# Seven block products for the MLP's first matrix product, and its output sums kept in DRAM

## The chip, the cores and the metric

The kernel runs on one core of a Trainium2 chip. A core has five engines with an instruction queue each: TensorE (PE in the profile, with its weight loads shown as PEld), VectorE (DVE), ScalarE (ACT), GpSimd (POOL) and SyncE (SP), which issues the transfers. Each queue is worked off strictly in order. TensorE reads on-chip memory (SBUF) and adds its results up in PSUM, which has eight banks; VectorE and ScalarE empty these. Transfers between DRAM and SBUF run on 16 DMA engines. The metric is the time of one execution on the device, in microseconds (us).

## The reference

The input x is 2048 rows of 576 numbers. With xn the layer-normalised x, the output is

```
x + Cr @ (xn @ Dr^T) - Ci @ (xn @ Di^T) + relu(xn @ w1) @ w2
```

where Cr, Ci (2048 x 2048) and Dr, Di (576 x 576) are cosine and sine matrices that come as inputs, w1 is 576 x 4608 and w2 is 4608 x 576. All is in single precision. The last term is called the MLP here: `xn @ w1` its first products, `relu(...) @ w2` its second products.

## The kernel before

Single precision is made from half precision: each operand is split into a high and a low float16 part, and a product is three matmuls (high x high, high x low, low x high). `split` (L164) makes the two parts, the high one on ScalarE (L166), the low one on VectorE (L167), after a scaling by a power of two that is found from the largest magnitude (`magnitude`, L97; `power`, L101, which sends it through GpSimd's `partition_all_reduce`, L105).

The 2048 rows are four groups g of 512 (xT[g] holds the transposed, split xn of one group), the 4608 hidden columns are nine blocks b of 512. A step n is one pair (b, g), in the order of `steps` (L604): all four groups of block 0, then of block 1, and so on. In step n the kernel computes the first products of (b, g) and, woven between them, the second products of the step before.

- First products (L305, `mlp1_step`): four PSUM tiles of 128 hidden columns by 512 rows. Each takes 13 matmuls that stream 512 columns (L292), and four matmuls of 64 rows (L317) do the remainder of the depth 576 = 4 x 128 + 64. `mlp1_out` (L325) empties the tiles of two such products into h: the four blocks of 128 x 256 after relu, and four sums of them (S1 to S4), each as high and low part.
- Second products (L347, `mlp2`): the 2 x 2 blocks of each product are multiplied as seven block products instead of eight (Strassen's scheme in Winograd's form, the table `PRODUCTS`, L269). Each has 12 matmuls that stream 288 columns (L357), into two PSUM tiles of pool ps2. After each of the seven, VectorE adds the PSUM tile, scaled, to the sums in SBUF (L363, tiles acc, which began as x itself, so that the residual is in them). After block 8 the sums go to DRAM (tiles spill), and come back when the output is put together (L853).
- Preparation of the next block is a list of small pieces that `work` (L607) takes one by one between the products: loads of w1 and w2, magnitudes, splits, and the sums of w2's blocks (L440).
- `passes` (L676) take the largest magnitudes of the sequence matrices, one 512 KB load and one ScalarE pass (L672) at a time, in the MLP's steps.

In block 0 the groups are also normalised (`normalize`, L221), their low parts are taken on GpSimd (`remainder`, L229) and transposed on TensorE (`transposes`, L238). After the MLP follow the two DFT stages: `dft1` (L747) and the loop from L857, with seven block products too. They take some 440 us and are not touched, but for how the sums are loaded.

Instructions are written in program order; a scheduler orders each engine's queue and places the waits. `issue_after` pins an instruction behind another one of the same engine. Pools hand out buffers: a tile is written only when the one that had the buffer before has been read for the last time.

## Time and profile before

| | |
|---|---|
| median of 3 runs | 1283.71 us (1282.86 to 1283.82) |
| the profiled execution | 1283.83 us, of which the span of instructions is 1282.0 us |
| PE busy | 1264.8 us, 99% |
| DVE busy | 980.5 us, 76% |
| ACT busy | 539.0 us, 42% |
| POOL busy | 36.5 us, 3% |
| mean granted TensorE clock | 0.997 of full speed |

How to read the profile: a row of groups has the line, the engine and operation, output<-inputs, shapes and count, then busy time in us and the mean of one in ns, and behind the bar the idle time before them and who ended it. A row of a timeline has start, duration (both us), engine, line, operation and count, and in brackets the idle time before it with its releaser. Operations of one engine overlap, so what one costs in a queue is the distance from start to start, which is a little less than its duration. In rows of stretches the columns are the stretch, its length, the busy time (with the number of instructions) of PE, PEld, DVE, ACT and POOL, the granted clock, the DMA share and GB/s.

### The profile page before, as it was taken

How to read it: one execution, taken by the hardware profiler on the slowest of the kernel's cores; microseconds unless marked ns; L12 is line 12 of the kernel's file. 1: busy time of each engine (PE TensorE's matmuls, PEld its weight loads, DVE VectorE, ACT ScalarE, POOL GpSimd, SP SyncE). 2: the span in 40 equal slices, each digit the busy share in tenths (PEclk: the TensorE clock that was granted, in tenths of full speed). 3: DMA queues.
4: the chain of work that ended last, by engine and by line, in shares of the span. 5: the costliest groups of instructions: out<-in, count | busy, mean ns of one | idle time of the engine just before them, and what ended most of it. 6: DMA issues, size and time to landing. Idle time of an engine off the chain costs nothing.

```text
span 1282.0 us, 21851 instructions
## 1 busy us (share of the span) xinstructions
PE 1264.8 (99%) x9164; PEld 859.2 (67%) x9164; DVE 980.5 (76%) x1671; ACT 539.0 (42%) x794; POOL 36.5 (3%) x60
## 2 busy tenths in 40 slices
PE   8799999999999999999999999999999999999998
PEld 7565665666565665666565665677777777777777
DVE  8978877786686687777867868568678788888875
ACT  5834443343443443434434434244443333333332
POOL 2310000000000000000000000000000000000000
PEclk8999999999999999999999999999999999999999
DMA  6102112221221222122222213330033435334320
GB/s 243 43 1 68 56 59 91 86 77 65 87 91 68 64 79 68 69 91 87 69 73 86 97 57 110 112 132 17 1 114 124 155 101 167 121 125 133 130 85 19
DMA packets 38002, 112.75 MB, mean 88 GB/s; under 512 B 3984, under 2 KB 10640, under 8 KB 37904
## 3 DMA queue, kind: packets, MB, share of 16 engines
q1 hardware_dynamic: 37904, 111.36, 25.9%
q8 instruction: 71, 1.16, 0.4%
q14 instruction: 27, 0.22, 0.0%
HBM read 101.91 MB, written 9.44 MB: 87 GB/s over the span
## 4 chain that ended last, share of the span: by engine, by line
PE 91%; DVE 5%; ACT 1%; DMA 1%; issue 1%; SPq 0%; POOL 0%; POOLq 0%; ACTq 0%; DVEq 0%
PE p L292 29%; PE p L357 27%; PE p L872 26%; PE pd L760 7%; PE p L317 1%; DVE acc L363 1%; DVE w2s L167 1%; DVE xn L226 0%; DVE w1s L167 0%; DMA acc<-in_x_dram 0%; DVE st L184 0%; DMA c<-in_cre_dram 0%; DVE h L336 0%; PE pd L770 0%; ACT xn L227 0%
## 5 line engine op out<-in xcount | busy, mean ns | idle before, releaser
L292 PE MATMUL p<-xT,w1s 128*128 128x512 f16 (+1 forms) x2136 | 434.7, 355 | 1.3 <-ACT xT L249 1.1
L357 PE MATMUL p<-w2s,h 128*128 128x288 f16 x3024 | 394.6, 286 | 2.0 <-ACT xT L252 1.0
L357 PEld LDWEIGHTS <-h 128*128 128x128 f16 x3024 | 295.3, 98 | 103.0 <-issue 2.8
L872 PE MATMUL p<-R,cs 128*128 128x288 f16 x2688 | 329.4, 286 | 0.0
L292 PEld LDWEIGHTS <-w1s 128*128 128x128 f16 x2136 | 193.5, 98 | 201.9 <-issue 18.4
L872 PEld LDWEIGHTS <-cs 128*128 128x128 f16 x2688 | 263.0, 98 | 66.3
L363 DVE SCALAR_TENSOR_TENSOR acc<-p,c_ub,acc 128x576 f32<-128x576 f32 x252 | 204.8, 813 | 39.0 <-PE p L357 38.5
L166 ACT ACTIVATE cs<-c,sc_c 128x1024 f16<-128x1024 f32 x112 | 128.5, 1148 | 200.2 <-PE p L872 147.5
L167 DVE SCALAR_TENSOR_TENSOR cs<-c,sc_c,cs 128x1024 f16<-128x1024 f32 x112 | 143.7, 1283 | 50.3 <-ACT cs L166 50.1
L336 DVE SCALAR_TENSOR_TENSOR h<-p,h 128x256 f16<-128x256 f32 (+1 forms) x144 | 79.8, 555 | 94.8 <-ACT h L335 94.5
L342 ACT ACTIVATE h<-s 128x1024 f16<-128x1024 f32 x72 | 76.1, 1057 | 160.5 <-DVE s L340 160.4
L335 ACT ACTIVATE h<-p 128x256 f16<-128x256 f32 (+1 forms) x144 | 69.9, 486 | 147.2 <-PE p L292 141.4
L343 DVE TENSOR_TENSOR h<-s,h 128x1024 f16<-128x1024 f32 x72 | 88.1, 1224 | 31.2 <-ACT h L342 30.2
L760 PE MATMUL pd<-dsp,xT 128*128 128x288 f16 x832 | 104.0, 286 | 0.2
L760 PEld LDWEIGHTS <-xT 128*128 128x128 f16 x832 | 80.7, 98 | 22.6 <-issue 2.5
L878 DVE SCALAR_TENSOR_TENSOR o<-p,us_c,o 128x288 f32<-128x288 f32 x112 | 57.6, 514 | 20.3 <-PE p L872 20.3
L672 ACT ACTIVATE f<-f 128x1024 f32<-128x1024 f32 x64 | 66.6, 1041 | 3.7 <-DMA f<-in_cre_dram 3.7
L332 ACT ACTIVATE s<-p 128x256 f32<-128x256 f32 x72 | 27.4, 380 | 74.0 <-PE p L317 54.5
L166 ACT ACTIVATE w2s<-raw_w,c_sw 128x576 f16<-128x576 f32 (+1 forms) x54 | 44.2, 851 | 25.9 <-DVE raw_w L445 15.4
L167 DVE SCALAR_TENSOR_TENSOR w2s<-raw_w,c_sw,w2s 128x576 f16<-128x576 f32 (+1 forms) x54 | 48.5, 916 | 7.6 <-ACT w2s L166 7.6
L167 DVE SCALAR_TENSOR_TENSOR w1s<-raw_w,c_sw,w1s 128x640 f16<-128x640 f32 x36 | 30.8, 892 | 9.8 <-ACT w1s L166 9.8
L166 ACT ACTIVATE w1s<-raw_w,c_sw 128x640 f16<-128x640 f32 x36 | 27.9, 817 | 24.0 <-DVE c_sw L109 23.6
(106 smaller groups left out, 672.5 us busy)
## 6 DMA issues: line engine op xcount, KB each, us to landing
f<-in_cre_dram SPq DMA_DIRECT2D x32, 512.0 KB, 3.5
f<-in_cim_dram SPq DMA_DIRECT2D x32, 512.0 KB, 3.5
c<-in_cre_dram SPq DMA_DIRECT2D x32, 512.0 KB, 4.0
c<-in_cim_dram SPq DMA_DIRECT2D x32, 512.0 KB, 4.6
raw_w<-in_w_dram SPq DMA_DIRECT2D x17, 640.0 KB, 4.0
raw_w<-in_w_dram SPq DMA_DIRECT2D x18, 576.0 KB, 3.8
acc<-in_x_dram SPq DMA_DIRECT2D x16, 288.0 KB, 7.4
spill<-acc SPq DMA_DIRECT2D x16, 288.0 KB, 2.5
```

Source lines behind the costliest of these rows:

```text
L166: nc.scalar.activation(hi, src, AF.Copy, scale=s)
L167: nc.vector.scalar_tensor_tensor(lo, src, s, hi, ALU.mult, ALU.subtract)
L292: nc.tensor.matmul(ps[:, cols], w1s[b, i // 2][:, hl, i % 2 * KT + k], xT[g][:, kx, cols], start=(start and n == 0), stop=(stop and n == l ...
L335: nc.scalar.activation(hi, src, AF.Relu)
L336: stt(lo, src, 0.0, hi, ALU.max, ALU.subtract)
L342: order["s"] = nc.scalar.activation(hi, st[:, 1:], AF.Copy).ins
L343: order["lo"] = nc.vector.tensor_tensor(lo, st[:, 1:], hi, ALU.subtract).ins
L357: nc.tensor.matmul(ps[:, c], h[:, x, qa, c * P : (c + 1) * P], w[:, y, qb], start=first and i == 0 and j == 0, stop=i == NQ - 1 and j == 2 ...
L363: order["acc"] = nc.vector.scalar_tensor_tensor(o, ps, us[b], o, ALU.mult, ALU.add).ins
L672: nc.scalar.activation(f, f, AF.Abs, scale=2.0**-10, accum_out=sums_c[:, n, q : q + 1])
L760: nc.tensor.matmul(ps[j], xT[g][:, kx, c * P : (c + 1) * P], dsp[j][:, hl, k], start=(t % 2 == 0 and n == 0), stop=(t % 2 == 1 and n == le ...
L872: nc.tensor.matmul(ps, w[:, a, k], r[:, c, rq], start=first and k == 0 and j == 0, stop=k == HK - 1 and j == 2, skip_group_check=not first,)
```

## The change

First products of blocks 1 to 8 (`pair_products`). Both operands are cut into 2 x 2 blocks: w1's 256 hidden columns of a product pair by halves of the depth 512 (blocks of 256 x 128), xT[g] by halves of the depth and of the rows (256 x 256). Seven products P1 to P7 of these blocks stand for the eight. Each is 6 matmuls that stream 256 columns; four of the seven (P2, P5, P3, P4) carry two more for the depth remainder. They add up in four PSUM banks that stay allocated: u (one for each of the two pairs of a step), v and w. Between them ScalarE copies intermediate values to SBUF (P1, P6, P5) and VectorE adds them (P2, P7, P3); relu, the low parts and the sums S1 to S4 follow as each block is complete. The order of the 14 products and of the seven second products in a step is written out in a list.

Sums of operands. Four sums of xT[g]'s blocks are made once for each group by `sums_x`: 14 tensor operations on GpSimd (128 x 512 elements), four conversions on ScalarE, in steps 2 to 5, into the memory of acc[g], whose contents have by then gone to DRAM. Five sums of w1's blocks are made for each half block by `sums_w1` on VectorE, and `split_w1b` splits 17 tiles of 128 columns where there were 10. The w1 buffers and the normalisation's buffers share one fixed tile (dbuf).

Sums of second products. After block 0 the sums are stored to DRAM. From block 1 on each step's four output blocks are started in one of three SBUF buffers (`sumbufs`, used in turn) by a scaled copy on ScalarE (second products 0, 2, 3 and 6, counted from 0), VectorE adds the other three (1, 4, 5), and a transfer issued by GpSimd adds the finished block to the one in DRAM: four for each step.

```diff
+    P1, P2, P6, P5, P7, P3, P4 = range(7)
+    LEFT = (0, 2, 8, 15, 13, 10, 5)
+    REST = {P2: (4, 0), P5: (7, 1), P3: (12, 1), P4: (7, 0)}
...
+    def sums_x(g):
+
+        f = mlp.tile([P, 2, 2, GH], F32, tag="first", name=f"t{g}", bufs=1)
+        tt = nc.gpsimd.tensor_tensor
+        for q, (head, tail) in enumerate((
+            ((0, 1), (0, 0)), ((1, 1), None), ((1, 0), None), ((1, 1), (0, 1)),
+        )):
+            t = f[:, q % 2]
+            h, l = halves(g, head)
+            if tail:
+                h2, l2 = halves(g, tail)
+                tt(t, h, h2, ALU.subtract)
+                tt(t, t, l2, ALU.subtract)
+            else:
+                tt(t, h, f[:, 1 - q % 2], ALU.subtract)
+            tt(t, t, l, ALU.add)
+            yield
+            hi, lo = (xsums[g][:, q, n] for n in range(2))
+            nc.scalar.activation(hi, t, AF.Copy)
+            yield
+            tt(lo, t, hi, ALU.subtract)
...
+        def product(n):
+            ps = {P2: v, P5: w, P3: w}.get(n, u)
+            first = n in (P1, P2, P5)
+            x, ws, a = right(g, n), w1s[b, i], LEFT[n]
+            todo = [
+                (ws[:, y, a + k], x[z][:, k]) for k in range(2) for y, z in ((1, 0), (0, 0), (0, 1))
+            ]
+            if n in REST:
+                k, c = REST[n]
+                todo += [(ws[:, y, k], xT[g][:, KM, (H1, H2)[c]]) for y in range(2)]
+            for m, (l, r) in enumerate(todo):
+                nc.tensor.matmul(
+                    ps, l, r, start=first and m == 0, stop=m == len(todo) - 1,
+                    skip_group_check=not first,
+                )
+
+        def value(q, src):
+            hi, lo = h[:, 0, q], h[:, 1, q]
+            nc.scalar.activation(hi, src, AF.Relu)
+            stt(lo, src, 0.0, hi, ALU.max, ALU.subtract)
+
+        def behind(n):
+            if n == P1:
+                nc.scalar.activation(c11, u, AF.Copy)
+            elif n == P2:
+                tt(c11, v, c11, ALU.add)
+                value(A11, c11)
+            elif n == P6:
+                nc.scalar.activation(s1, u, AF.Copy)
+            elif n == P5:
+                nc.scalar.activation(c22, w, AF.Copy)
+            elif n == P7:
+                tt(c22, u, c22, ALU.add)
+                value(A22, c22)
+            elif n == P3:
+                tt(r21, w, s1, ALU.add)
+                nc.scalar.activation(r21, r21, AF.Relu)
+                stt(s3, c11, 0.0, r21, ALU.max, ALU.subtract)
+                stt(s1, c22, 0.0, r21, ALU.max, ALU.add)
+                stt(s2, c22, 0.0, s3, ALU.max, ALU.subtract)
+            elif n == P4:
+                value(A12, u)
+                stt(s4, u, 0.0, s2, ALU.max, ALU.subtract)
+                hi, lo = (h[:, k, S1 : S4 + 1] for k in range(2))
+                order["s"] = nc.scalar.activation(hi, st[:, 1:], AF.Copy).ins
+                order["lo"] = nc.vector.tensor_tensor(lo, st[:, 1:], hi, ALU.subtract).ins
...
-        o = accs[g].rearrange("p (h c) (j e) -> p h j c e", h=2, j=2)[:, row, col]
-        order["acc"] = nc.vector.scalar_tensor_tensor(o, ps, us[b], o, ALU.mult, ALU.add).ins
-        if b == NB - 1 and n == 6:
-            for t in range(g * TG, (g + 1) * TG):
-                nc.sync.dma_start(spill[t], acc[t])
+        blocks = accs[g].rearrange("p (h c) (j e) -> p h j c e", h=2, j=2)
+        o = sums[row, col] = sums[row, col] if b else blocks[:, row, col]
+        if b and n in (0, 2, 3, 6):
+            o = sums[row, col] = sumbufs[next(turns) % len(sumbufs)]
+            nc.scalar.activation(o, ps, AF.Copy, scale=us[b])
+        else:
+            order["acc"] = nc.vector.scalar_tensor_tensor(o, ps, us[b], o, ALU.mult, ALU.add).ins
+        if b and n not in (0, 2, 3):
+            nc.gpsimd.dma_start(spill[g, row, col], o, accum_op=ALU.add)
+        if b == 0 and n == 6:
+            for r in range(2):
+                for j in range(2):
+                    nc.sync.dma_start(spill[g, r, j], blocks[:, r, j])
...
+    def sums_w1(b, i):
+        r = raws["w1", b, i]
+        a11, a12, a21, a22 = (r[:, k : k + 2] for k in (0, 2, 5, 7))
+        tt = nc.vector.tensor_tensor
+        tt(a22, a21, a22, ALU.add)
+        tt(a21, a11, a21, ALU.subtract)
+        tt(a11, a22, a11, ALU.subtract)
+        tt(a12, a12, a11, ALU.subtract)
+        tt(r[:, 4], r[:, 4], r[:, 9], ALU.subtract)
...
+        if b:
+            first, second = (pair_products(b, g, i) for i in range(NQ))
+            m = lambda q: mlp2(pb, pg, q)
+            for k, (do, q) in enumerate((
+                (first, P1), (first, P2), (m, 0), (first, P5), (first, P6), (m, 1), (second, P1),
+                (first, P7), (m, 2), (second, P2), (first, P3), (first, P4), (m, 3), (second, P6),
+                (m, 4), (second, P5), (second, P7), (m, 5), (m, 6), (second, P3), (second, P4),
+            )):
+                do(q)
+                if k % 2:
+                    work()
+                if n < 6:
+                    k % 2 or next(tq, None)
+                elif k in (5, 11, 20) and (k != 5 or n % 3 == 0) and passes:
+                    passes.pop(0)()
+            continue
```

More of the change, by code (lines that the diff above doesn't have):

```diff
@@ L288 @@
     w1s, w2s, us, hs = {}, {}, {}, {}
+    w1bufs = [mlp.tile([P, W1B], F32, name=f"w1buf{i}", bufs=1) for i in range(2)]
+    w1bufs += [dbuf[:, i * W1B : (i + 1) * W1B] for i in range(2)]
     def mlp1_group(b, g, i, cols, ps, wk=WK, start=True, stop=True):
@@ L347, in mlp2 @@
+    places, sums = {}, {(r, j): None for r in range(2) for j in range(2)}
+    turns = itertools.count()
+    sumbufs = [mlp.tile([P, 2, EH], F32, name="sum0", bufs=1)] + [
+        dbuf[:, k : k + 2 * EH].rearrange("p (c e) -> p c e", e=EH)
+        for k in (2 * W1B, 2 * W1B + 2 * EH)
+    ]
     def mlp2(b, g, n):
@@ L627, in new_d @@
         nonlocal dsp
-        dsp = [dpool.tile([P, 2, KT, EH], F16, tag="d", name=f"dsp{j}") for j in range(4)]
+        dsp = [d.bitcast(F16).rearrange("p (n k e) -> p n k e", n=2, k=KT) for d in dbufs]
     def split_d(j):
@@ L677 @@
     passes.append(lambda: sum_c(4 * len(units) - 1))
+    tq = itertools.chain(*(sums_x(g) for g in range(NG)))
     for n in range(2, len(steps)):
@@ L695 @@
                 weave(stats([(g + 1) * TG + i for i in range(TG)]))
+        if b == NB - 1 and g == 1:
+            w = mlp.tile([P, 2, 7, EH], F16, tag="w2s", name="sums", bufs=4)
+            w = w.rearrange("p n q e -> p (n q e)").bitcast(F32)
+            sumbufs[:] = [
+                w[:, k * 2 * EH : (k + 1) * 2 * EH].rearrange("p (c e) -> p c e", e=EH) for k in range(3)
+            ]
+        if b:
[14 more added lines that the diff above has]
+            continue
         ps = []
@@ L710 @@
                 todo += prepare_block(1)
-            for _ in range(1 if b else 3):
+            for _ in range(3):
                 work()
@@ L714 @@
                 mlp2(pb, pg, q)
-            for _ in range(1 if b else 3):
+                for _ in range(2 if q > 3 and n == 2 or q < 2 and n == 3 else n - 2):
+                    next(tq, None)
+            for _ in range(3):
                 work()
-            if n > 3 and i % 2 and passes:
-                passes.pop(0)()
     while todo:
@@ L852, in load_out @@
         for h in range(2):
-            nc.sync.dma_start(o[:, h], spill[p + h * NP])
+            g, c = divmod(p + h * NP, TG)
+            for col in range(2):
+                nc.sync.dma_start(o[:, h, col * EH : (col + 1) * EH], spill[g, c // 2, col][:, c % 2])
     AHEAD = 3
```

71 lines of the change are left out of this document (61 added, 10 removed).

## The prediction

> **What bounds the kernel now.** I read the page first (engines, chain of waits), then PE's timeline inside the MLP, then stretches of one step each, then VectorE's, ScalarE's and GpSimd's queues.
>
> ```profile
> span 1282.0 us, 21851 instructions
> PE 1264.8 (99%) x9164; PEld 859.2 (67%) x9164; DVE 980.5 (76%) x1671; ACT 539.0 (42%) x794; POOL 36.5 (3%) x60
> PE 91%; DVE 5%; ACT 1%; DMA 1%; issue 1%; SPq 0%; POOL 0%; POOLq 0%; ACTq 0%; DVEq 0%
> ...
> 304.62 0.60 PE L317 MATMUL p<-xT,w1s 64*128 64x512 f16 x4
> 305.15 2.98 PE L292 MATMUL p<-xT,w1s 128*128 128x512 f16 x13
> 307.97 3.10 PE L357 MATMUL p<-w2s,h 128*128 128x288 f16 x24
> 310.91 2.97 PE L292 MATMUL p<-xT,w1s 128*128 128x512 f16 x13
> ...
> 326.77 0.60 PE L317 MATMUL p<-xT,w1s 64*128 64x512 f16 x4
> ...
> 304.62:326.77 22.15, 22.15 (x141) 13.34 (x141) 16.09 (x29) 8.25 (x14) 0.35 (x1) 1.00 0.24 76
> 326.77:348.92 22.15, 22.15 (x141) 13.33 (x140) 15.97 (x29) 9.16 (x16) 0.35 (x1) 1.00 0.23 77
> 348.92:371.07 22.15, 22.15 (x141) 13.33 (x140) 18.29 (x40) 12.44 (x19) 0.37 (x1) 1.00 0.10 35
> 371.07:393.22 22.15, 22.15 (x141) 13.34 (x140) 15.41 (x25) 6.96 (x14) 0.00 (x0) 1.00 0.36 120
> ```
>
> TensorE is the bound: 99% busy, 91% of the chain. Inside the MLP it never stops, at full clock (1.00): a step lasts 326.77 - 304.62 = 22.15 us in each stretch. 13 matmuls of 512 columns take 307.97 - 305.15 = 2.82 us, 217 ns each; 24 of 288 columns 310.91 - 307.97 = 2.94 us, 122.5 ns; the four remainder ones 0.53. So 52 x 0.217 + 0.53 + 84 x 0.1225 = 11.28 + 0.53 + 10.29 = 22.10. VectorE is busy 15.4 to 18.3 us of a step, ScalarE 7 to 12.4: both have room, the third step of a block (row 348.92, w2's preparation) least.
>
> **The matmuls.** Each of the 32 steps of blocks 1 to 8 loses its 52 + 4 first-product matmuls and gets 2 x (7 x 6 + 4 x 2) = 100 of 256 columns. The line through 122.5 ns at 288 and 217 at 512 gives 109 ns at 256: 10.90 us instead of 11.81. The start of the kernel has rows for the weight side:
>
> ```profile
> 10.26 1.47 PE L524 MATMUL p<-xn 128*128 128x256 f16 x12
> 11.67 1.72 PE L292 MATMUL p<-xT,w1s 128*128 128x128 f16 x28
> 13.23 0.38 PE L524 MATMUL p<-xn 128*128 128x256 f16 x2
> ```
>
> 28 matmuls of 128 columns, each with weights of its own, follow every (13.23 - 11.67)/28 = 56 ns, so a load per 109 ns does not bind. The 256-column fillers came every 1.41/12 = 117 ns; that is my upper end. I take 109, as the nearer rows are the MLP's own. A step becomes 10.90 + 10.29 = 21.19 us, 0.96 less than the measured 22.15; 32 steps: **-30.8 us** (upper end: 0.8 us less for each step, -5).
>
> **VectorE and ScalarE in a step.** Costs in the queue, start to start:
>
> ```profile
> 398.03 0.41 DVE L338 SCALAR_TENSOR_TENSOR s<-p,s 128x256 f32<-128x256 f32 x1
> 398.36 0.41 DVE L339 SCALAR_TENSOR_TENSOR s<-p,s 128x256 f32<-128x256 f32 x1
> 398.70 0.81 DVE L363 SCALAR_TENSOR_TENSOR acc<-p,c_ub,acc 128x576 f32<-128x576 f32 x1
> 399.42 0.41 DVE L340 SCALAR_TENSOR_TENSOR s<-p,s 128x256 f32<-128x256 f32 x1
> 401.20 1.22 DVE L343 TENSOR_TENSOR h<-s,h 128x1024 f16<-128x1024 f32 x1
> 402.33 0.81 DVE L99 TENSOR_REDUCE c_mf<-raw_w 128x1 f32<-128x640 f32 x1
> 403.18 0.15 DVE L382 TENSOR_REDUCE c_mw<-c_mf 128x1 f32<-128x2 f32 x1
> 403.51 0.35 POOL L105 PARTITION_ALL_REDUCE top<-c_mw  x1 [51.76 <-DVE c_mw L382]
> 448.29 1.12 DVE L167 SCALAR_TENSOR_TENSOR w2s<-raw_w,c_sw,w2s 128x864 f16<-128x864 f32 x1 [1.08 <-ACT w2s L166]
> 449.33 0.81 DVE L363 SCALAR_TENSOR_TENSOR acc<-p,c_ub,acc 128x576 f32<-128x576 f32 x1
> 450.06 0.45 DVE L444 TENSOR_TENSOR raw_w<-raw_w 128x288 f32<-128x288 f32 x1
> 450.42 0.81 DVE L363 SCALAR_TENSOR_TENSOR acc<-p,c_ub,acc 128x576 f32<-128x576 f32 x1
> 393.67 0.38 ACT L332 ACTIVATE s<-p 128x256 f32<-128x256 f32 x1 [2.36 <-PE p L317]
> 393.95 0.38 ACT L335 ACTIVATE h<-p 128x256 f16<-128x256 f32 x1
> ```
>
> VectorE: 256 elements 0.33 us, 576 0.72, 1024 1.13, 288 within SBUF 0.36, the 864-wide split 1.04; ScalarE: 256 elements 0.28. Four of seven L363 sums go to ScalarE (-2.9). Behind each pair stand ten 256-wide VectorE operations instead of five and one of 512 (about 0.6): 2 x 1.05 = +2.1. w1's split grows from 2560 to 4352 columns a block (1.2 ns each by the 864-wide row: +2.2), its sums add ten small ones (about 3.2): +1.35 a step. VectorE goes from 16.4 (mean of the four stretches) to some 17.0 of 21.2 us, 80%. ScalarE gets seven 256-wide operations a pair for two and one of 512 (+1.9 a step), four copies of 576 (about 0.6 each: +2.4) and +0.6 for the split: from 9.2 to some 14.5. Neither becomes the bound by its sum; in strict order their waits for each other count too. The built queue gives the tightest place: VectorE's sum of second product 4 must be done before second product 6. TensorE has 18.0 - 7.3 = 10.7 us between the end of pair one's P7 and that product. In a block's third step VectorE's queue holds there, besides the sum itself (0.72): two 864-wide splits (2.1), ten 256-wide operations (3.3), eight scale operations of 0.15 behind POOL's reduction (1.2), four sums of 0.36 (1.4) and the 1.13 low part: 9.1 us. That leaves 0.9 us for the hand-overs from ScalarE, which each of these splits and low parts waits for. I allow 1 us lost in each of seven blocks, **+7** (ends: 0 and 2 us, 14). The other steps do without the w2 pieces and have more room: 0.
>
> **POOL.** 14 tensor operations for each group, 56 in all, stand in its queue in steps 2 to 5, ahead of the scale reductions and the first adding transfers.
>
> ```profile
> 42.03 0.99 POOL L231 TENSOR_TENSOR xn<-xn 128x64 f16<-128x64 f32 x1 [3.39 <-ACT xn L227]
> 42.98 1.38 POOL L234 TENSOR_TENSOR xn<-xn 128x512 f16<-128x512 f32 x1
> 44.33 0.52 POOL L231 TENSOR_TENSOR xn<-xn 128x64 f16<-128x64 f32 x1
> 43.26 1.42 DVE L444 TENSOR_TENSOR raw_w<-raw_w 128x288 f32<-128x288 f32 x1
> 44.71 0.46 DVE L445 TENSOR_TENSOR raw_w<-raw_w 128x288 f32<-128x288 f32 x1
> ```
>
> One takes up to 1.4 us, a group about 19: less than a step, so each group's sums, which start when its acc has been stored, are ready before its first use a step and more later. Five of group 0's stand ahead of remainders of block 0, at a place where POOL had 3.4 us to spare (row 42.03). But VectorE's L444 took 1.42 us beside L234, and the same operation alone 0.46 (L445 behind it): it ended only with POOL's. In steps 4 and 5 some 28 such operations meet VectorE operations with two SBUF inputs, most of the new ones: up to 28 x 0.96 = 27 us of VectorE time, of which 2 x 4.2 us is free; and ScalarE's conversions wait for POOL inside its queue. Ends 0 and 18; I take **+6**, a third, because POOL waits for the group's store between groups and half of the meetings fall into idle time. [...]
>
> **The adding transfers.** 8 x 16 = 128 of 288 KB, issued by POOL.
>
> ```profile
> spill<-acc SPq DMA_DIRECT2D x16, 288.0 KB, 2.5
> o<-spill SPq DMA_DIRECT2D x16, 288.0 KB, 3.2
> ```
>
> No adding transfer is in this trace. A plain store lands in 2.5 us, a load in 3.2; reading and writing one after the other give 5.7. POOL's issue is not shown: between its 0.35 us reduction and 1.38 us operation. So 2.9 to 7.1; I take 5, between them. The critical buffer: the block finished by second product 5 (TensorE 18.0, VectorE's sum about 19 to 20) must have landed before ScalarE starts the next step's second product 0 (3.0, that is 24.2): 4.2 to 5.4 us. A later landing holds ScalarE, and behind it the copies for P5 and P6 (0.6 + 2 x 0.28) that P7 needs at 27.85; so TensorE stops only beyond 6.3 to 7.5 us. At 5: 0; at 7.1: 0 to 0.8 us a step, +25. The other three buffers have some 12 us or more.
>
> **No cost.** w1's later splits belong to the next block and have a step or more. SP gets 16 more, half as large, loads at the end, each beside some 20 us of matmuls. dbuf's fixed slots keep the order of four buffers.
>
> **Sum.** 1283.83 - 30.8 + 7 + 6 = **1266 us**. The profiled execution is 0.12 us above the median of the runs (1283.71), so the sum stands for the median as well.
>
> **Rivals.**
> - All covers hold: 1283.8 - 30.8 = 1253. For: TensorE was never kept waiting in any of the four stretches. Against: the 0.9 us above, and the SBUF meeting.
> - The adding transfer becomes the wait: a landing of over about 6.9 us costs 0.55 us a step, which eats the 17.8 us; at 7.5, some 1.2 us a step late, 1266 + 37 = 1303. For: the 5.7 of two passes plus an issue; against: the rows are of transfers that share the engines with 512 KB loads and still land in 2.5.
> - VectorE's chain is the bound in every step, not one in four: more than 0.6 us a step beyond my sum and the gain is gone; 1 us gives 1266 + 25 = 1291. For: ScalarE and VectorE now hand over about twice as often. Against: 4 us of room.
> - 256-column matmuls come every 117 ns: 1283.8 - 5 + 13 = 1292.
>
> **Numbers.** Forecast (gain partly eaten, 1258 to 1276) 0.50; full gain 0.20; late adding transfer 0.13; VectorE's chain 0.13; slow matmuls 0.04. What a measurement can tell from no change is about 0.2%, 2.6 us. Slower: nearly all of the last three, less the milder half of VectorE's: 0.23; same 0.04; faster 0.73. The range reaches from the full gain to 1292, which leaves out the worst landing times; the forecast's own range is 1258 to 1276.
>
> **What would show it.** Right: matmuls of 256 columns every 109 ns; steps of 21.2 us with TensorE idle about 1 us in a block's third step, before second product 6, released by VectorE's sum; adding transfers landing in 4 to 6 us; idle TensorE and long VectorE operations between 100 and 165 us. Wrong: TensorE idle at P7 or P6 in each step, behind ScalarE's scaled copy that a transfer released; or VectorE busy above 18 us of each step.

## The result, and the profile after

| | before | after |
|---|---|---|
| median, us | 1283.31 (4 runs, 1282.86 to 1283.82) | 1366.15 (4 runs, 1357.50 to 1374.03) |
| ratio | | 1.0644 [1.0579, 1.0709] |
| profiled execution, us | 1283.83 | 1367.02 |

The change made the kernel 6.4% slower. The forecast was 1266 us. First the page of the changed kernel, its span, engines and chain:

```profile
span 1364.9 us, 25952 instructions
PE 1270.6 (93%) x10572; PEld 1023.3 (75%) x10572; DVE 1030.5 (76%) x1911; ACT 725.1 (53%) x1226; POOL 221.1 (16%) x244
PE 43%; issue 18%; DVE 16%; DMA 11%; ACT 6%; POOL 4%; SPq 0%; POOLq 0%; ACTq 0%; DVEq 0%
```

The chain is TensorE's for 43% where it was for 91%. Two subtractions divide the loss. TensorE was idle for 1364.9 - 1270.6 = 94.3 us, before for 1282.0 - 1264.8 = 17.2: +77.1. It was busy for 1270.6 us where 30.8 us of matmuls less should have left 1234.0: +36.6, which no step of the forecast had; what it is made of stands in the last section. 77.1 + 36.6 - 30.8 = 82.9, the growth of the span. Most of the 36.6 is a lower clock: the mean granted clock fell from 0.997 to 0.974.

Stretches of single steps follow (steps 4, 5, 8, 9 and 10, counted from 0; columns as in the prediction):

```profile
140.10:177.70 37.60, 27.00 (x188) 19.88 (x187) 35.00 (x59) 15.46 (x29) 19.45 (x15) 0.82 0.21 61
177.70:209.00 31.30, 25.13 (x186) 19.56 (x184) 26.59 (x50) 14.87 (x29) 16.35 (x14) 0.89 0.33 79
255.20:276.50 21.30, 21.30 (x187) 18.00 (x185) 17.37 (x40) 14.59 (x28) 3.04 (x5) 1.00 0.50 97
276.50:302.80 26.30, 23.01 (x187) 18.77 (x185) 18.67 (x42) 15.25 (x30) 3.61 (x5) 0.94 0.59 129
302.80:326.90 24.10, 21.54 (x187) 18.00 (x185) 17.55 (x44) 17.84 (x34) 4.73 (x7) 1.00 0.55 116
```

Step 8 is the step that was forecast: 21.3 us, TensorE never idle, VectorE 17.4 (forecast 17.0) and ScalarE 14.6 (14.5). Steps 4 and 5, with GpSimd busy for 19 and 16 us, take 37.6 and 31.3. Between them stand steps such as 9 and 10 that lose 3 to 5 us each, one of them at a clock of 0.94. By the starts of the steps in the trace, block 0 is 18.5 us longer than before (step 4 starts at 140.1 instead of 121.6), steps 4 to 6 take 93.8 us instead of 66.5, steps 7 to 35 670.6 instead of 642.4, and what follows the MLP 460.4 instead of 451.6.

TensorE's timeline in the clean step, and the adding transfers' row of the page (KB each, us to landing):

```profile
264.29 1.91 PE L435 MATMUL bank<-xT,w1buf 128*128 128x256 f16 x16
266.04 0.82 PE L435 MATMUL bank<-acc,w1buf 128*128 128x256 f16 x6
...
spill<-dbuf POOLq DMA_DIRECT2D x74, 288.0 KB, 5.1
```

16 matmuls of 256 columns take 266.04 - 264.29 = 1.75 us, 109 ns each, as forecast; and the adding transfer lands in 5.1 us, where 5 was taken. So the two figures that seemed least sure were right, the landing at least in its median. Timelines of the changed kernel show two kinds of place where the time was lost. In the rows up to 202.81 (block 0, step 4, step 5) GpSimd's sums of xT stand in the way, in the last four (steps 12 and 13) the adding transfers:

```profile
95.03 0.63 ACT L407 ACTIVATE acc<-t 128x512 f16<-128x512 f32 x1 [2.94 <-POOL t L404]
...
153.49 2.73 DVE L615 TENSOR_TENSOR raw_w<-raw_w 128x288 f32<-128x288 f32 x2
154.66 1.25 POOL L400 TENSOR_TENSOR t<-xT 128x512 f32<-128x512 f16 x1
157.58 0.78 ACT L180 ACTIVATE w2s<-raw_w,c_sw 128x576 f16<-128x576 f32 x1 [6.19 <-DVE raw_w L616]
161.45 0.81 DVE L618 TENSOR_TENSOR raw_w<-raw_w 128x288 f32<-128x288 f32 x2
163.69 1.44 PE L435 MATMUL bank<-acc,dbuf 128*128 128x256 f16 x6 [7.42 <-ACT s L452]
...
202.81 0.38 POOL L119 PARTITION_ALL_REDUCE top<-c_mw  x1 [7.27 <-issue]
...
367.98 0.88 POOL L511 DMA_DIRECT2D spill<-sum  x1 [8.52 <-DVE sum L509]
370.37 1.76 POOL L511 DMA_DIRECT2D spill<-dbuf  x2 [1.51 <-DVE dbuf L509]
378.74 0.74 ACT L507 ACTIVATE dbuf<-p,c_ub 128x576 f32<-128x576 f32 x1 [2.86 <-DMA spill<-dbuf]
380.08 0.81 PE L435 MATMUL bank<-acc,dbuf 128*128 128x256 f16 x6 [2.32 <-ACT s L452]
```

ScalarE waits for GpSimd in its own queue (95.03). Two VectorE sums of w2's pieces take 2.73 us while GpSimd works and 0.81 once it has ended (161.45); ScalarE waits for them with the copies for P6 behind it, and TensorE for 7.42 us. At 202.81 GpSimd stands still for 7.27 us ahead of a scale reduction and waits for nothing that this view shows (the last section has more). At 368 to 380, three adding transfers are issued within 4.2 us; the buffer that ScalarE needs at 375.9 for second product 0 comes back at 378.7, 8.3 us after its transfer was begun (the first of the two at 370.37, by the order of the code); and P7 is held by the very path that the prediction's rival of a late transfer described.

### The profile page after: what moved, and what is told of

The parts are those of the page before. It is cut to its first block, busy times and chain, and to the rows that moved or that the text cites. A ratio compares the mean times of both kernels' runs of the same rounds, so it can differ in the third digit from the quotient of the medians.

```text
span 1364.9 us, 25952 instructions
## 1 busy us (share of the span) xinstructions
PE 1270.6 (93%) x10572; PEld 1023.3 (75%) x10572; DVE 1030.5 (76%) x1911; ACT 725.1 (53%) x1226; POOL 221.1 (16%) x244
## 3 DMA queue, kind: packets, MB, share of 16 engines
q1 hardware_dynamic: 42256, 111.36, 25.1%
q0 software_dynamic: 18432, 37.76, 19.9%
## 4 chain that ended last, share of the span: by engine, by line
PE 43%; issue 18%; DVE 16%; DMA 11%; ACT 6%; POOL 4%; SPq 0%; POOLq 0%; ACTq 0%; DVEq 0%
PE p L1072 23%; PE p L498 7%; PE pd L958 6%; PE bank L435 6%; DMA spill<-dbuf 4%; DVE w2s L181 2%; POOL spill L511 2%; DMA spill<-sum 2%; DMA f<-in_cim_dram 2%; ACT f L846 1%; DVE h L443 1%; DMA c<-in_cre_dram 1%; DMA f<-in_cre_dram 1%; ACT j L585 1%; DVE h L469 1%
## 5 line engine op out<-in xcount | busy, mean ns | idle before, releaser
L498 PE MATMUL p<-w2s,h 128*128 128x288 f16 x3024 | 423.8, 293 | 28.9 <-DVE sum L509 9.3
L498 PEld LDWEIGHTS <-h 128*128 128x128 f16 x3024 | 302.1, 100 | 112.1 <-issue 32.5
L435 PEld LDWEIGHTS <-dbuf 128*128 128x128 f16 x1600 | 158.5, 99 | 48.5 <-issue 24.8
L435 PEld LDWEIGHTS <-w1buf 128*128 128x128 f16 x1600 | 157.2, 98 | 40.2 <-issue 18.6
L181 DVE SCALAR_TENSOR_TENSOR cs<-c,sc_c,cs 128x1024 f16<-128x1024 f32 x112 | 143.7, 1283 | 46.8 <-ACT cs L180 46.7
L435 PE MATMUL bank<-acc,dbuf 128*128 128x256 f16 x768 | 107.7, 277 | 21.0 <-ACT s L452 20.8
L435 PE MATMUL bank<-acc,w1buf 128*128 128x256 f16 x768 | 105.9, 275 | 15.7 <-ACT s L452 15.6
L511 POOL DMA_DIRECT2D spill<-dbuf x74 | 66.4, 922 | 331.7 <-DVE dbuf L509 327.7
L435 PE MATMUL bank<-xT,dbuf 128*128 128x256 f16 x832 | 112.3, 276 | 0.9 <-DVE s L466 0.9
L435 PE MATMUL bank<-xT,w1buf 128*128 128x256 f16 x832 | 110.4, 274 | 0.7 <-ACT acc L454 0.7
L958 PE MATMUL pd<-dbuf,xT 128*128 128x288 f16 x832 | 104.3, 286 | 1.6 <-DVE R L987 1.3
L507 ACT ACTIVATE dbuf<-p,c_ub 128x576 f32<-128x576 f32 x74 | 54.4, 735 | 50.8 <-PE p L498 23.7
L846 ACT ACTIVATE f<-f 128x1024 f32<-128x1024 f32 x64 | 66.9, 1045 | 14.6 <-DMA f<-in_cim_dram 9.6
L443 DVE SCALAR_TENSOR_TENSOR h<-acc,h 128x256 f16<-128x256 f32 x128 | 55.4, 433 | 25.1 <-ACT h L442 22.8
```

The costliest lines, as they stand in the source:

```text
L181: nc.vector.scalar_tensor_tensor(lo, src, s, hi, ALU.mult, ALU.subtract)
L435: nc.tensor.matmul(ps, l, r, start=first and m == 0, stop=m == len(todo) - 1, skip_group_check=not first,)
L443: stt(lo, src, 0.0, hi, ALU.max, ALU.subtract)
L498: nc.tensor.matmul(ps[:, c], h[:, x, qa, c * P : (c + 1) * P], w[:, y, qb], start=first and i == 0 and j == 0, stop=i == NQ - 1 and j == 2 ...
L511: nc.gpsimd.dma_start(spill[g, row, col], o, accum_op=ALU.add)
L846: nc.scalar.activation(f, f, AF.Abs, scale=2.0**-10, accum_out=sums_c[:, n, q : q + 1])
```

## The experiments

**Four causes, one edit each.** The buffers dealt in another order:

```diff
-            o = sums[row, col] = sumbufs[next(turns) % len(sumbufs)]
+            k, q = divmod(next(turns), 4)
+            k = k % 2 * 2
+            o = sums[row, col] = sumbufs[(k, 1, 2 - k, k)[q]]
```

> Same work; the buffers are dealt so that a step's second product 0 takes the buffer of the step before's second product 3 (whose transfer starts after second product 4) instead of that of second product 2 (whose transfer starts after second product 5). Theory T (in steps 7 to 35 TensorE is held because an adding transfer hands its buffer back too late): most of the 24.7 us that TensorE waits at L435 behind ScalarE's copies goes, and the half-rate windows that follow such stops with it; steps 7 to 35 take about 645 us instead of 670.6, and the whole about 1335 to 1345. Rival V (VectorE's sum of second product 4 comes late, and all transfers are issued late because of it): the waits only change places, the whole stays at 1360 to 1370.

Measured: 1338.86 us (1.0433 [1.0409, 1.0458]), 27.3 less than the change as it was. (The changed kernel's own interval, 1.0579 to 1.0709, is 8 us to either side, and so is that of each difference against it.) Theory T holds. The groups from 190 to 905 us, of the changed kernel and then of this one (busy, mean of one in ns, idle before them and who ended it):

```profile
L498 PE MATMUL p<-w2s,h 128*128 128x288 f16 x2584 | 358.5, 291 | 19.9 <-DVE sum L509 9.3 <-DVE dbuf L509 7.6 <-DVE c_sw L123 2.9
L435 PE MATMUL bank<-acc,w1buf 128*128 128x256 f16 x768 | 105.9, 275 | 15.7 <-ACT s L452 15.6
L435 PE MATMUL bank<-acc,dbuf 128*128 128x256 f16 x702 | 96.1, 273 | 9.1 <-ACT s L452 8.9
```

```profile
L498 PE MATMUL p<-w2s,h 128*128 128x288 f16 x2664 | 362.7, 287 | 18.9 <-DVE sum L511 13.8 <-DVE dbuf L511 3.6 <-DVE c_sw L123 1.3
L435 PE MATMUL bank<-acc,w1buf 128*128 128x256 f16 x768 | 104.7, 272 | 5.1 <-ACT s L452 4.7 <-DVE s L459 0.5
L435 PE MATMUL bank<-acc,dbuf 128*128 128x256 f16 x706 | 96.8, 273 | 4.1 <-ACT s L452 4.1
```

The stops behind ScalarE's copies fall from 24.5 to 8.8 us; those of the second products (L498), nearly all behind VectorE, stay at 19 to 20.

Plain stores, and no transfers at all:

```diff
-            nc.gpsimd.dma_start(spill[g, row, col], o, accum_op=ALU.add)
+            nc.gpsimd.dma_start(spill[g, row, col], o)
```

> GpSimd issues the same 128 transfers as plain stores, without adding (the sums of blocks 1 to 8 are left out of the output). Theory T with the landing time as its cause: a plain store lands in about 3 us instead of 5.1, so the stops behind ScalarE's copies go nearly all: about 1335. Rival (the late issue on GpSimd, or VectorE's order, is the cause and the landing time is not): 1355 to 1370.

```diff
-        if b and n not in (0, 2, 3):
-            nc.gpsimd.dma_start(spill[g, row, col], o, accum_op=ALU.add)
```

> The 128 adding transfers are left out (so are the sums of blocks 1 to 8 in the output); copies and VectorE's sums stay. Theory T: no buffer is waited for, the stops behind ScalarE's copies are gone, those of second product 6 behind VectorE (17 us) stay: steps 7 to 35 take about 635 us, the whole is 1325 to 1335. Rival (second product 6 waits for VectorE only because ScalarE's queue was held by transfers): steps 7 to 35 come down to 615 to 620 us, the whole to 1310.

Measured: 1327.21 and 1329.77 us. Leaving the transfers out is worth 36 us, and 27 of these come from the other dealing of the buffers alone. Theory T's figure for e4_notransfer is met, and the 15 us for which second products still wait behind VectorE there are VectorE's own, as no transfer is left. e2_store misses its 1335 on the fast side. e1_swap still costs some 10 us more than these two; that is what the adding transfers cost even with the better dealing.

The sums of xT left out:

```diff
-        x = xsums[g][:, {P5: 0, P6: 1, P4: 2, P7: 3}[n]]
-        return x[:, 0], x[:, 1]
+        return halves(g, {P5: (0, 0), P6: (0, 1), P4: (1, 0), P7: (1, 1)}[n])
...
-    tq = itertools.chain(*(sums_x(g) for g in range(NG)))
+    tq = iter(())
```

> The sums of xT's blocks are left out: no tensor operations on GpSimd and no conversions, and P4 to P7 read the blocks of xT themselves. [...] Rival (they cost about the 6 us of the forecast, the rest of the loss comes from the weights' preparation in dbuf and the order of steps 4 to 6): about 1355.

Measured: 1320.90 us, 45.3 less; the rival's 1355 is missed by 34. Step 4 starts at 121.1 us (the change: 140.1; before: 121.6), steps 4 to 6 take 69.8 (the change: 93.8; before: 66.5). So the sums of xT cost what block 0's last steps and steps 4 to 6 had lost.

**Do they add up, and what is left?**

> Both edits together: the sums of xT's blocks left out (as in e3_nox, with P4 to P7 reading xT's blocks themselves) and the buffers dealt in the other order (as in e1_swap). If the two causes are separate, their gains add up: 1366.2 - 45.3 - 27.3 = about 1294. Rival (the late transfers were partly an effect of GpSimd's sums, or the stops share the same place): 1305 to 1320.

It is both diffs above. Measured: 1301.07 us (1295.87 to 1304.31): 65 of the 73 us, nearer to the theory's 1294 than to the rival. The causes are separate but for some 7 us, which is within the interval of the changed kernel's median. What was left was not spread evenly. Of the 29 steps from 7 on, the nine with n % 3 = 0 were 0.3 to 4.3 us longer than others of their place in the block. They have a third pass over the sequence matrices, which the change added because steps 4 and 5 have none. The next kernel deals two a step from step 4 on (and leaves the sums of xT out too):

```diff
-                if n < 6:
-                    k % 2 or next(tq, None)
-                elif k in (5, 11, 20) and (k != 5 or n % 3 == 0) and passes:
+                if k in (11, 20) and passes:
```

> e5_nox_swap with the passes over the sequence matrices dealt as in the kernel before: two a step from step 4 on, and no third one in every third step. Theory F (in e5_nox_swap the steps with a third pass are 0.3 to 4.3 us longer than their like, some 18 us together: ScalarE waits in its queue for the 512 KB load, and its pass of 1.2 us stands ahead of the copies for P6 and P7): 1301 - 15 to 18 = 1283 to 1286. Rival C (these steps are long because the queues of VectorE and ScalarE are near their limit anyway, and two passes in steps 4 and 5 cost as much): 1295 to 1303.

Measured: 1282.24 us, ratio 0.9988 [0.9979, 0.9998]; 18.8 us less than e5_nox_swap. Theory F holds, a little better than its 1283 to 1286. How a third pass costs, in ScalarE's and TensorE's timelines of e5_nox_swap:

```profile
655.16 1.06 ACT L847 ACTIVATE f<-f 128x1024 f32<-128x1024 f32 x1
656.12 0.19 ACT L847 ACTIVATION_READ_ACCUMULATOR f<-f 128x1 f32 x1
656.21 0.36 ACT L451 ACTIVATE s<-bank 128x256 f32<-128x256 f32 x1
656.63 0.82 PE L434 MATMUL bank<-xT,w1buf 128*128 128x256 f16 x6 [2.80 <-ACT s L451]
```

The pass stands ahead of the copy that P7 waits for. And the one regular stop that e9_passes still has, 1.56 us in each block's third step (seven of them, 10.9 us; VectorE's row, then TensorE's, whose bracket has 1.40 because the profile lets the matmul before it end 0.16 us after the next could start):

```profile
536.00 0.82 DVE L510 SCALAR_TENSOR_TENSOR sum<-p,c_ub,sum 128x576 f32<-128x576 f32 x1
536.88 1.63 PE L497 MATMUL p<-w2s,h 128*128 128x288 f16 x12 [1.40 <-DVE sum L510]
```

That is the prediction's step on VectorE, in its place, with its wait, at 1.56 instead of 1 us.

**Can VectorE's stop be moved away?** Second product 6 behind P3 and P4 (on top of e1_swap):

```diff
-                (m, 4), (second, P5), (second, P7), (m, 5), (m, 6), (second, P3), (second, P4),
+                (m, 4), (second, P5), (second, P7), (m, 5), (second, P3), (second, P4), (m, 6),
```

> e1_swap, with second product 6 moved behind the second pair's P3 and P4 in the written list, so that VectorE has 1.75 us longer for its sum of second product 4. Theory O (the 18.8 us that TensorE waits at L498 for VectorE in e1_swap are a matter of the place in the list): nearly all of it goes, 1320 to 1325. Rival (VectorE as a whole is late by then, and TensorE waits at the next product instead): 1333 to 1342.

Measured: 1345.14 us, 6 more than e1_swap. Theory O fell: between 190 and 905 us, TensorE's 18.9 us at L498 went to 0.5, but it waited 14.9 us for the copies of P6 (8.8 in e1_swap), 10.1 for those of P5 (0.7) and 7.4 for VectorE's sum of P7 (none) instead. The order of the list was not the cause; the queue is late as a whole.

**What makes the sums of xT dear?** The conversions off ScalarE:

```diff
-            nc.scalar.activation(hi, t, AF.Copy)
+            nc.gpsimd.tensor_copy(hi, t)
```

> e1_swap, with the 16 conversions of the sums' high parts moved from ScalarE to GpSimd, so that ScalarE's queue has nothing that waits for GpSimd. Theory Q (most of the 45 us of the sums of xT is the crossing of the two in-order queues): 1300 to 1310, and step 4 starts near 125 us. [...]

Measured: 1342.30 us against 1338.86. Theory Q fell; ScalarE's waits for GpSimd, though plain in the timeline, were not what cost. Then the same operations on VectorE:

```diff
-        tt = nc.gpsimd.tensor_tensor
+        tt = nc.vector.tensor_tensor
```

> e1_swap with the 56 tensor operations of the sums of xT on VectorE, in the same places; GpSimd has none. [...] Rival W (VectorE has no room for 34 us more in steps 2 to 5 either): 1330 to 1350.

Measured: 1326.02 us, 13 less than on GpSimd, and still 25 more than with none (e5_nox_swap). Rival W's 1330 to 1350 is missed on the fast side. The starts of the steps divide the price: step 4 begins at 120.6 us instead of e1_swap's 139.6, so block 0 lost its 19 us to GpSimd; steps 4 to 6 take 93.4 us instead of 92.7, where they have 71.0 without the sums. There it is the place that costs, whichever engine does the work. So the place was changed: seven products only from block 2 on, so that block 1 has VectorE's old load, and the sums spread over steps 4 to 10, on GpSimd:

```diff
-        if b:
+        if b > 1:
             first, second = (pair_products(b, g, i) for i in range(NQ))
...
-                if n < 6:
-                    k % 2 or next(tq, None)
-                elif k in (5, 11, 20) and (k != 5 or n % 3 == 0) and passes:
+                if n < 11:
+                    k % 4 or next(tq, None)
+                elif k in (5, 11, 20) and passes:
...
```

> e6_reorder with seven block products only from block 2 on: block 1's first products are eight as before (four steps of 22.15 instead of 21.19 us, +3.8), the sums of xT are spread over steps 4 to 10, and their conversions are on GpSimd. Theory (what the sums cost was their place: block 0's last steps and a VectorE that had no room): the 45 us go but for 5 to 10, about 1285 to 1290. Rival (each of GpSimd's 56 operations takes about a microsecond from VectorE wherever it stands, and the steps have no room for it): 1300 to 1315.

Measured: 1377.89 us, the slowest of all. It has two edits that cost by themselves (e6_reorder's list, and a third pass in every step from 11 on), but block 1 lost 27 us in two stretches alone (36.0 and 35.0 us below, where a step has 22.15), in a way that the theory did not have (GpSimd's timeline, and one row of VectorE's):

```profile
158.37 1.16 POOL L404 TENSOR_TENSOR t<-t,xT 128x512 f32<-128x512 f32 x1
165.49 0.38 POOL L119 PARTITION_ALL_REDUCE top<-c_mw  x1 [5.96 <-issue]
165.90 0.15 DVE L122 TENSOR_SCALAR half<-top 128x1 f32<-128x1 f32 x1 [14.46 <-POOL top L119]
...
192.16 0.67 POOL L407 CAST acc<-t 128x512 f16<-128x512 f32 x1
200.51 1.59 POOL L409 TENSOR_TENSOR acc<-t,acc 128x512 f16<-128x512 f32 x1 [7.67 <-issue]
```

VectorE had its input for the reduction ready at 149.6 and got the answer at 165.9: 10 us behind GpSimd's sums, and 6 us in which GpSimd did nothing between its last tensor operation and the reduction. Going back to tensor operations cost it 7.67 us once more. To tell this queue from the slowing of VectorE's own operations beside GpSimd's (1.42 us instead of 0.46 in the prediction's rows), the reductions of block 2 went to TensorE, as the kernel does it for blocks 0 and 1, with GpSimd's sums as they were:

```diff
-        if b > 1:
+        if b > 2:
             yield from power(s, p, mx["w1", b][:, i : i + 1])
...
```

> e8_block2, with the three scale reductions of block 2 done on TensorE as in blocks 0 and 1, so that nothing waits for GpSimd's sums in steps 4 to 7. Theory queue (VectorE stood idle behind reductions that stood behind GpSimd's sums): steps 4 to 7 of block 1 take about 95 us instead of 127, the whole about 1345 to 1350. Rival port (the sums slow VectorE itself): 1365 to 1378.

Measured: 1353.92 us, 24 less, a little short of theory queue's figure (its 127 us for block 1 had counted 11 us of block 0 in). The stretches from step 5's first second product to step 6's, and on to step 7's, in e8_block2 and then in e15_pe_scales:

```profile
157.50:193.50 36.00, 23.92 (x142) 13.90 (x141) 20.30 (x36) 9.51 (x16) 16.55 (x16) 0.86 0.14 33
193.50:228.50 35.00, 24.09 (x140) 13.98 (x140) 19.18 (x41) 15.86 (x26) 7.54 (x8) 0.90 0.40 75
```

```profile
158.70:186.80 28.10, 24.08 (x143) 13.88 (x142) 24.17 (x39) 10.43 (x17) 20.27 (x18) 0.94 0.36 83
186.80:209.50 22.70, 22.70 (x145) 13.36 (x144) 15.27 (x35) 12.40 (x21) 3.33 (x4) 1.00 0.44 78
```

36.0 and 35.0 us become 28.1 and 22.7 (before: 22.2). So most of what GpSimd's sums cost here was what stood behind them. In the 28.1 that stay VectorE is busy for 24.2 us, and TensorE's one stop, 4.02 us, is for a sum of VectorE's. An operation of VectorE that reads two tiles in SBUF, beside GpSimd's operations and after their end at 175.5 us:

```profile
163.21 2.18 DVE L359 TENSOR_TENSOR h<-s,h 128x1024 f16<-128x1024 f32 x1
175.81 1.23 DVE L359 TENSOR_TENSOR h<-s,h 128x1024 f16<-128x1024 f32 x1 [1.12 <-ACT h L358]
```

So this rest is, at least in part, VectorE's own operations taking longer beside GpSimd's, 2.18 us instead of 1.23 here.

**Does the adding cost anything by itself?** All first products as eight blocks, with the copies, the adding transfers and e1_swap's dealing:

```diff
-        if b:
+        if False:
             first, second = (pair_products(b, g, i) for i in range(NQ))
...
```

> One part of the change alone: first products as eight blocks in all nine w1 blocks, as before, but the sums of second products kept in DRAM with copies on ScalarE and the 128 adding transfers, buffers dealt as in e1_swap. Theory (adding transfers cost nothing when each has a step's third to land, and VectorE and ScalarE have room): 1283 to 1288. Rival (the copies on ScalarE and the landing cost something in any schedule): 1292 to 1305.

Measured: 1297.63 us. The rival has the time, the theory has the steps: a step, and what follows the MLP in this kernel, and the same place before.

```profile
147.90:170.10 22.20, 22.20 (x142) 13.39 (x141) 13.72 (x26) 12.66 (x22) 4.15 (x5) 1.00 0.60 130
833.40:863.40 30.00, 25.11 (x201) 18.91 (x200) 10.55 (x21) 11.31 (x17) 4.77 (x6) 0.99 0.65 145
```

```profile
830.50:860.50 30.00, 29.61 (x242) 22.81 (x241) 19.68 (x36) 9.99 (x17) 0.40 (x1) 1.00 0.40 147
```

From block 1 to block 7 TensorE never stops, at 22.15 us a step. The loss lies at the end of the MLP: TensorE is busy 25.1 of 30 us there instead of 29.6, while ScalarE's first copy of the DFT stage waits for the last adding transfer, whose buffer's memory is handed on:

```profile
854.10 0.50 ACT L977 ACTIVATE c<-pd,c_rho 128x288 f32<-128x288 f32 x1 [5.85 <-DMA spill<-sums]
```

The last step's buffers in acc of group 2 instead:

```diff
+        if n == len(steps) - 1:
+            sumbufs[:] = [
+                flat[2][:, k * 2 * EH : (k + 1) * 2 * EH].rearrange("p (c e) -> p c e", e=EH) for k in range(3)
+            ]
```

> e11_half, with the last step's three output buffers in acc of group 2, which the DFT stage writes later. Theory: the 9 us that e11_half needs more after the MLP are the wait of the DFT stage's first copies for the last adding transfers: 1288 to 1291. Rival (the end has another cause): 1296 to 1299.

Measured: 1293.79 us, between the two expectations. That wait is a part, about 4 us. ScalarE then waits 6.65 us for the first load of a sequence matrix and starts at 853.95 us; before, it starts at 848.84, 4.9 us behind that load's issue at 843.99. What held the load here was not tried; the rest stays open.

**All together.** e1_swap's dealing, block 1 with eight products, two passes a step, w2's pieces spread, and the sums of xT divided:

```diff
-        tt = nc.gpsimd.tensor_tensor
+        tt = (nc.vector if g else nc.gpsimd).tensor_tensor
...
-                for _ in range(2 if q > 3 and n == 2 or q < 2 and n == 3 else n - 2):
+                if n == 3 or b and q < 6:
                     next(tq, None)
...
-        steps += [lambda i=i: (split_w2(b, i, 0), sums_w2(b, i)) for i in range(NQ)]
         for i in range(NQ):
+            steps += [lambda i=i: (split_w2(b, i, 0), sums_w2(b, i))]
             steps += [lambda: None] * 2
...
```

> Seven block products from block 2 on, buffers as in e1_swap, two passes a step, the pieces of w2 spread further, the sums of xT of group 0 on GpSimd in steps 3 and 4 and of groups 1 to 3 on VectorE up to step 8. By the separate causes: 1301 (e5_nox_swap) - 16 (passes) - 7 (w2's pieces) + 3.8 (block 1 with eight) + 5 to 12 (the sums of xT) = 1287 to 1294. If the causes are not separate: 1305 or more.

Measured: 1287.11 us, ratio 1.0025 [1.0014, 1.0036]: the causes add up, at the low end of the 1287 to 1294. Next, VectorE for all four groups, from step 4 on, and e16_half_end's buffers:

```diff
-        tt = (nc.vector if g else nc.gpsimd).tensor_tensor
+        tt = nc.vector.tensor_tensor
...
-                if n == 3 or b and q < 6:
+                if b and q < 7:
                     next(tq, None)
...
```

> e12_all, with all four groups' sums of xT on VectorE in steps 4 to 8 (none on GpSimd) and the last step's three output buffers in a part of acc that the DFT stage writes later. If GpSimd's sums of group 0 cost the 7 us that step 3 of e12_all was longer than before, and the last transfers the 5 to 9 us after the MLP: 1287 - 7 - 5 = about 1275. If VectorE has no room in steps 4 to 8, or the end has another cause: 1283 to 1288.

Measured: 1284.11 us, 0.9998 [0.9988, 1.0008]. With no sums on GpSimd, the stretch from step 2's to step 3's second products came down from 30.6 us (at a clock of 0.94) to 25.1 (at 1.00; before: 23.8), but what follows the MLP did not get shorter in this kernel. A stretch of block 1 with some 12 of VectorE's 56 operations in it:

```profile
149.90:172.10 22.20, 22.20 (x142) 13.38 (x141) 22.20 (x45) 14.17 (x26) 4.48 (x5) 1.00 0.55 128
```

VectorE is busy for the whole stretch, and TensorE doesn't stop once: here the sums are free, at a place where the products leave VectorE time.

```diff
             lambda: later(p) if b else next(p, None),
-        ]
+        ] + [lambda: None] * (3 if b > 1 else 0)
```

> e13_end, with w2's splits and sums three places later in the list, so that they fall behind second product 6 of a block's third step. Theory: the 1.56 us that TensorE waits in each third step of a block (some 11 us) are VectorE's queue of w2 pieces ahead of its sum of second product 4; they go, and the time is 8 to 11 us below e13_end. Rival: the pieces then hold second product 4 or a copy in the fourth step, and the time is within 3 us of e13_end.

Measured: 1282.79 us, 0.9989 [0.9980, 0.9998]. The 1.56 us in each third step are gone, and 1.33 come in each fourth: the rival, but for 1.3 us, which is no more than the intervals of the two. The last kernel moves w2's pieces one place further and puts the loads of the last stage in another order:

```diff
-        if kh == 0 and p + 1 < NP:
-            load_out(p + 1)
         if n + 1 < len(units):
             load_c(n + 1)
+        if kh == 0 and p + 1 < NP:
+            load_out(p + 1)
...
```

> e14_w2, with w2's pieces one place later again, and with the second unit's loads of the sequence matrices ahead of the second loads of the sums in SyncE's queue. If both remaining stops go: 7 x 1.3 + 3 = 12 us less, about 1271 to 1274; if only the loads' order helps: 1279; if both stops come back elsewhere: 1281 to 1284.

Measured: 1280.64 us, ratio 0.9969 [0.9958, 0.9981]: 0.3% faster than the kernel before. Of the two edits only the loads' order shows in the trace (TensorE's stops at that place fall from 2.0 to 0.9 us); the fourth step's stop stays. Its third, fourth and next first step of a block:

```profile
342.20:363.40 21.20, 21.20 (x186) 17.94 (x184) 16.48 (x40) 16.70 (x32) 3.87 (x5) 1.00 0.56 118
363.40:386.30 22.90, 21.56 (x186) 18.02 (x185) 16.62 (x34) 13.19 (x28) 4.84 (x6) 1.00 0.78 177
386.30:407.60 21.30, 21.30 (x187) 18.01 (x186) 17.63 (x40) 14.35 (x28) 3.03 (x6) 1.00 0.49 98
```

## Why the prediction was wrong, step by step

| step of the prediction | forecast, us | measured, us | by |
|---|---|---|---|
| the matmuls | -30.8 | -30.8 | 109 ns; clean steps of 21.2 to 21.3 |
| VectorE's queue in each third step | +7 (0 to 14) | +10.9 | 7 x 1.56 in e9_passes |
| GpSimd's sums of xT | +6 (0 to 18) | +45.3 | e3_nox |
| adding transfers | 0 (0 to 25) | +19.8 to 27.3 | e5 against e3; e1 against the change |
| passes over the sequence matrices | not there | +18.8 | e9 against e5 |
| the rest | 0 | about +18 | e9's remainder, below |

The rows come from a chain of runs, each with one cause less (the change, e3_nox, e5_nox_swap, e9_passes), and each has in it what its stops cost in clock. With 19.8 for the transfers they add up to 82, and the median grew by 82.8. The remainder: e9_passes is 1280.0 us of span where 1282.0 - 30.8 = 1251.2 was to be had; of these 28.8 us 10.9 are VectorE's stops, some 6 more lie in steps 4 to 6, 2.4 in the fourth steps (0.34 each), 2.7 in steps 33 and 34, 1.3 in clean steps of 21.28 instead of 21.19, and 5 behind the MLP.

- **The matmuls** were right: price, number and place.
- **VectorE's queue** was right in mechanism and place; the term was mis-sized by half a microsecond a block. (ScalarE's terms add up to 14.1 us a step, not to the 14.5 that stands there; 14.6 was measured.)
- **GpSimd's sums** are the step that failed most. The prediction bounded them by the slowing of VectorE's operations alone. That is there: 2.73 us for two operations beside GpSimd's instead of 0.81, some 0.96 us a meeting, just the price of the row it had quoted. But the 18 us came from counting meetings in VectorE's busy time, with two other costs left out. One is the queue: what stands behind the sums on GpSimd, and on VectorE behind the reductions (14.46 us in one place of e8_block2; 24 us for the three reductions in that kernel). The prediction named these reductions as queued behind the sums and put no price on it. The other is the place: on VectorE itself, with none of them on GpSimd, the sums cost 25 us in steps 2 to 5 (e10_vector), nearly all of it in steps 4 to 6, and none in a stretch with time to spare (e13_end). Whether a group's sums are ready before their first use was the wrong question; who waits meanwhile was the right one.
- **The adding transfers.** The landing time was right at the median, 5.1 for 5. The step that failed took the median for every transfer. Three are issued within some 4 us at the end of a step, and the landing runs from 4.0 to 10.3. "TensorE stops only beyond 6.3 to 7.5 us" was nearly right as a limit: in the second steps of five blocks the waited-for landing took 8.3 to 9.3 us and TensorE stopped for 2.3 to 3.3, which puts the limit at 6.0 (the prediction's own terms, 27.85 less 1.16 and 24.2 added to 4.2, would have given 6.7). The rival that used it (up to 1303) had the mechanism; it missed because one late landing in a block was not thought of, only a landing late in all. The price was mainly that of a buffer's turn, not of adding: e1_swap, which adds just as much, takes 27.3 of the 36 us back, and e11_half's steps of blocks 1 to 7 have no stop at all.
- **The passes** were not in the prediction, though its diff shows the condition `n % 3 == 0`. A step "moved" was not followed: the passes of steps 4 and 5 came back as a third one in every third step, ahead of the copies for P7.
- **"No cost"** for SyncE's queue at the end was wrong by a little: eight loads of half the size stand ahead of a 512 KB load, and TensorE stops there (2.0 us in e14_w2, 0.9 when the order is turned).
- **The chance** of "slower" was 0.23, in three rivals that each had one mechanism. Each of three causes left out or under-priced was by itself enough to eat more than half of the 30.8 us.

## What to carry to other kernels

When a kernel's bound engine is 99% busy, everything that was hidden behind it can become a bound of its own: ask for every moved operation what stands behind it in its queue, and take a transfer's worst landing, where three of them are issued together, not its median (10.3 us here, not 5.1). A step that repeats its work at another place is a moved step, and counts like one. A saving of 0.96 us a step is smaller than one late turn of a buffer or one pass in the wrong place; deal buffers so that the next user is the one whose transfer was issued first. Side work goes where the engine has time in that very stretch (here a fully busy VectorE cost nothing in block 1 with eight products, and 22 us in steps 4 to 6 with seven).

## What the runs showed of the hardware

**Half the clock behind TensorE's longer stops.** From 40 us on, the records of the granted clock in the changed kernel show 14 stretches at 0.5, of 3.4 to 10.2 us, 61.4 us in all; eight of them, of 3.4 us each, lie between 200 and 1100 us. By TensorE's matmul records it stopped 16 times for 2.01 us or more in that time: 14 of these stops stand just before a stretch at half rate, or reach into it, and two do not (2.39 us at 230.68, 2.32 at 380.08). None of its 12 stops of 1.28 to 1.91 us does. Two stops, on either side:

```profile
324.00 1.63 PE L498 MATMUL p<-w2s,h 128*128 128x288 f16 x12 [1.91 <-DVE dbuf L509]
...
436.52 0.93 PE L435 MATMUL bank<-acc,dbuf 128*128 128x256 f16 x6 [2.01 <-ACT s L452]
```

The first is followed by full rate, the second by 3.4 us at half (437.09 to 440.50), which cost another 1.7 us. That is the 36.6 us of too long busy time in the main: from 40 us on TensorE was busy for 54 us of the stretches at half rate, which makes 27, and before none were that late; what the other 10 are was not traced. The changed kernel's four runs spread by 16 us, those of before by 1, and the longer the run, the lower its mean clock (0.984 at 1357.5 us, 0.981 at 1365.3, 0.974 at 1367.0, 0.973 at 1374.0). Why it differs from run to run was not tried.

**GpSimd's standstill.** Between its tensor operations and a reduction over partitions, in either direction, GpSimd stood still for 7.27 us in the changed kernel (202.81 us) and for 5.96, 5.88 and 7.67 in e8_block2 (165.49, 191.90 and 200.51 us), and the views show nothing that it waited for. In the kernel before, the last tensor operation ends at 76.6 us; the next reduction has its input only at 137.9, and starts 0.15 us behind it. What GpSimd does in that time was not shown.

**Adding transfers.** One of 288 KB lands in a median of 5.1 us where a plain store of the same size took 2.6 in the changed kernel and 2.5 before, takes 0.86 us of GpSimd to issue, and the 128 took 19.9% of 16 engines' span, 2.1 us of all 16 for each. They took from 4.0 to 10.3 us; the longest are among three that were issued within some 4 us.
